# Batches 4, 5 and a tile of batch 3 turned to scoring all four experts, on a one-core state-read and expert-attention kernel

## The chip, the cores and the metric

The kernel runs on one core of a Trainium2 chip. The metric is the device time of one execution in microseconds (us). PE is the matrix engine, DVE the vector engine, ACT the scalar engine, POOL the general engine, and SP the engine on whose queue the DMA transfers are issued.

## The reference

Eight batches `x` of 8 heads, 512 tokens, 64 numbers each, and 32 state slots per head, are read against each other; the two results, 544 rows of 512 numbers per batch of which 512 are tokens, go through an attention layer with four experts, of which each row uses two.

```python
scores = scale * np.matmul(x, state.transpose(0, 1, 3, 2))   # tokens read the state
xread = np.matmul(softmax(scores), state)
scores2 = scale * np.matmul(state, x.transpose(0, 1, 3, 2))  # the state reads the tokens
sread = np.matmul(softmax(scores2), x)
x = concatenate([xread, sread])          # 8 batches, 544 rows, 512
logits = x @ w_gate                      # 4 experts, the 2 largest are kept
for e in range(4):
    q, k, v = x @ wq[e], x @ wk[e], x @ wv[e]
    a = softmax(causal(scale * (q @ k.T)))
    out += weight_of_e_for_this_row * (a @ v @ wo[e])
```

## The kernel before

The program is recorded first and emitted later. Each call to `st.mm`, `st.do`, `st.either` or `st.dma` records a step with the tiles that it reads and writes; `run` then emits all steps in the order that the constant `ORDER` holds, which also holds which of several engines does a step that more than one can do ("ways") and which buffer each tile gets. So nearly every instruction of the profile stands on one line, that of `run`, and is told apart by its tiles. On each engine instructions run in the order in which they were emitted. All transfers are issued on SP, before and after the change.

For each batch `front` makes, from tokens `xh` and their transposes `xT`, the scores against the state, softmax over 32 slots (`eb`, with maxima `mb` and sums `sbm`), its transposes `at`, the products `gs` of state and weights, and from these the values `v`, keys `kt`, queries and the weights of the gate (`wgt`). In batches 1 to 7 the softmax of the tokens comes from `state_scores`: two banks of PSUM (`sas`) hold all scores with tokens along a row, DVE turns them in blocks of 32 by 32 into `eb`, and the same banks give the state's own softmax `e2` with the maxima `m2`, which `side` goes on with (`a2`, `a2t`).

The causal attention of a batch works on four tiles of 128 tokens; tile `i` looks at `i + 1` blocks of 128 keys. `probs` does a unit of one or two tiles, in one of two ways:

- Sparse ("s"): each token has two slots, one for each expert that it uses. Queries are masked by slot into six columns of 64 (`m6`, `qf`, then a high and a low half-precision part in `qh`, turned by a DMA into `qm`). A tile has two lanes of scores. Each lane is the sum of a product over 128 rows of PE and one over 64 rows. `reads` multiplies each lane with the values of three experts (194 columns), weighs the result (`c`, `z`) and adds the slots' halves.
- Dense ("d", "0", "1"): all four experts are scored. Queries come out of PE already turned and are only split in two parts, `qm`. A tile has four lanes; a lane's products run over 64 rows, and two of them, on the upper and the lower half of PE, run side by side. `reads` multiplies each lane with one expert's values (65 columns), and a row's weight is zero for experts that it does not use.

In both, every product is made three times, of high and low parts. Each lane's scores go through DVE (a masked copy to `p` with its maximum `mx`), ACT (exponential), a split into `ph` (high part on ACT mostly, low part on POOL or DVE), a DMA that turns `ph` into `pt`, and `reads` on PE. Which way a tile goes is set by two numbers, `D1` and `DA`:

```python
def units_of(b):
    if b < CFG["D1"]:
        units = [((0, "s"), (1, "s")), ((2, "s"),), ((3, "s"),)]
    elif b < CFG["DA"]:
        units = [((1, "d"),), ((0, "s"), (2, "s")), ((3, "s"),)]
    else:
        units = [((1, "d"),), ((0, "0"), (2, "0")), ((0, "1"), (2, "1")), ((3, "0"),), ((3, "1"),)]
    return units
```

Before, both are 6: batches 0 to 5 are sparse, 6 and 7 dense. `tail` does the state's rows of two batches at a time, `result` the last product, of which the result leaves through `o`. `FILL` is a list of times at which a matmul on zeros (`band`) keeps PE at work in the first microseconds.

Of the kernel before, what the change touches and what calls it, by code (L numbers as in the profile page):

```python
# [21 lines left out]
ORDER = (
    (
        "c-jrs1A7n(7(n6AU$tu4EiBu{vTfV87nW_?wr$(CZR6hGaGvKqfshB%K{iMNksuWmg2<2_GC~oE00kivM1(|;8=^u6%nJYr1PlTS2_X%n$6S"
        "yMazI=Nf|aluih)6V2mps@um%!9bchGBAqFgk<xmb{LUD)#1uzfRfN)S2GC(XSh&ACjlz{S(1xrE&s0AUI6SCq7s0d{s8=izhSQ~O+VMqa$A"
        "U`C90&oiQVm_=4r{N4#fjV#wqCjbA2vy-M)P?hq6RW{as0Y>I0_4I*5FYBoMQ9AA;1V>4+_(oWLj!07`yoGGfo`x5u0mUA2`iu-WW<iJ8?s{"
        "y*adr`Gqi#u&>k}30cZlNpfxCMhRn#c4CZ48=mgDREA)WExD6KI7U&L%p&wj>BG?-iVrFOx*I@&MLLayR{b4aK!i~@u%Ht;ZLc`%Gtc3wE5s"
        "Kn55L$vGU?3F3xiAQpVi*+1o=^b?1JN=Z0+XR4?tr1N9DBhqSO+WcCQN|wkPoK7JXnccU^YyGRTz!BLJ6D-+hHV(hB+__ronvpOwnmNjDZDE"
        "3B%J&h(Tjv2F!v6I1Uy=1X_&?p(HlMdk{dCF(R#pHMj(-;987CO|T{|f~t5Q9zs)m1dZ@DM5e}A3Lii-ERA*XF+73iPz(3-GYF(=_y%r48N3"
        "Z&APPmLJ5Uzy!c%w))$s+C!*}o=YG7*E$F(s#e1MnG4Zp!hsE1#nBi2WwHuwoTqf>Hdj^E)kq=j(Q4(nhi?2bKf9k#_E&;t8mZw$pg*dKpFU"  # L30
        "pxo{uqO`0$v6oA(QgXF!Pp)r;t=eGf2bvPz@ZqEUcq`ChU0M~PC(#E*achREbNL?ur;Ql88{Ua&}<xzKj<$_!<qOC5>jf~fTQvM<Q$8B!yNn"
        "zBQOmG(R7SWV{jz?1H)06mj1w8+=S_9EXJj5G!6mNQyhwk@yHP|5ydCw#551X;ZNF({U|4e$0QUB4?zSBCBmc>8-wX92{UG=WV9V~(>4^`f&"
        "ti{lAvO8%104#0R5tGl!7ARR?I{B={xPfIJgs2QZC9syKo?7q}_M`<KiC7M0sg1=Ag)U7*66o%uE|)5FNxr7)Hv6F$?YG!E_YM(-DlwS;;sW"
        "R-$7Vi9;Yf??>n37>)z+G@inw7=Z(L4+molip=paIyUAwoD8F2R%pV39G6dE6&gYnC^<IeiWDDPQZqh-QMfdvz<7KPTTydPfUW5m$LFYgk~c"
        "|ZDo$rO8lU3A)P@pbN<7PFu`1odR9KDLQb{UG=lD1mp)yo}&SOd_MOok_w%}rPnuk*fx{U?tFyFyiRGlv2U93U(ur{^i)L4@`&=Iafudpn2q"
        "Pp}NL#Q6T!J$;2-eLn9Nv${t8&V^>jE(6EHlcPDo!iq@Y(_D77&WDibb>omb9#s6=mL(RYuJ-U(NTVng{TW1;1SfFdQk!%O=Br0C*yGx3>Wb"
        "rU&jd)i^o%I?n)DB67`^jJedx05O<^4oRWLf2mFYMI2GT(Db$Dd%T!9v)95_!k<^@m6Z1B?%<cFqrsE4doo?a`O2T_35nklJbd8hp6~4~j@C"
        "GlXnbd}R+a-R?!TgB#Ng95_SNRj($Miglo^o4`ipwZ1=aQY0TPkp<e#aGblk-S>UP%vdIpviYn1OHcDw<83D4(pQb@T&Q(@*@2b7;G)p)^>L"
        "f8l0YPY-dI?54z+k)QDfs>F|Q3*F|ev|BdI0V&IOcq8qhEwY`q%3jLBcexxt=X;!o^Gi<7!rSPe<mKO(7Q;(cE+9K-F71#AQh@i-A3Q)isXC"
        "YE`<#pOaW*c*^C+Se<m_CJ3v&qP<|6!pBTGTa#LuuO@26s1oJ(+iF3B%>7e$h)T#5svG|#8!ScWTeX0F2rsR~!)2mBZpP+hLUued%Rl83yIY"  # L40
        "Vs3&#|`+f)Z)+lo?ml_eB&c>P2O-r{)->DHh<xd{GE%!89FM*<PaU9<MNeH$S1x{jrb^?rNnxS&e3_gD*ZHxUYDf$50BFwIzeywq}-(+d`eE"
        "zVY){h_yYani*%n((G3aKLNZEKI`RX$DV_NbKcp^vi8`@MU%n+p<T7<-lb?K=!pRpLq^BjBcH^WHru}$`{^sr+%02lCB^RL48Z2j|j~107JX"
        "{M)GC@kNLv@V);}n`g`g5T4;6*e-QO-(A?Zqi&06(W;97P6lZ~puL)ECnrCW#^E<hG1dmj0R!i%A%tmlqUOVoEfLB`;}!W|a#vl!s|?c|{lH"
        "HKmh*8eL*b8tKDv<c`FZCG>_;X*>~$F9{^EB$OaYC6{EdCX&=LoHNT^Nh{gp1|^Zfd|A@VTY5wp<SLbvD{_+_Q${HvS!4v4l6Q2C9!hB`BQG"
        "$urq!{UT}E<QxhLf$lT77wI#J8ZBN?anC5JqbDVjzr$S5AokL5j8lqLLB#_I&lDV3zMEYPuBMW$+1c|z4>n)b5lGLDB?Q+Z0mZIUkK@jSwo@"
        "dRF|%XuPC*A+aCpUEw%A(OR}JdkGcTx!a6ZXqw_wJy>bI)j_bVvV3J<tcWN7xGG0@)DiN-(|4P)KHtnAE=d#;ej@Z+sb5K#Y=TI_m)A{R|B+"
        "-%;7iMS+3Jtox;zkt1Q!ZT1)!KT<#_xX*IW#)-p@q>ra`jKjgi%m)g?bKFdexD;;DFe~{PmMY_uy=^+tyj)qx3`6L_otNfBs8Dax0lJ=Kx@="
        "tzCPua*rt&c6_$XZAK$Z`dJE1S5ktk8GTQBeQNT3*DYo0;{4))UdbrfTXMPJ2l-UB}@yiq6&e8dX1PbPd$Fx`pFu3{9Z(xSuWNm^x2C>3m(O"
        "v2=|l)Yv-G*6V!UsH=2?9@DiNq+@N9)|XK>N*YK*IjLK8oXxS(c3R`;Y8_*9t&wcj(K1E`$atG6iFB+?wBy=X2Fe5*CtG!$?$h-=OPa_eyJ?"
        "^Gluou=c0zC4Y}v}`b&B1w{W?eP+IX2O6C_MB=_CE3gJm0U=ghi;Gw3`yq#5<G4w3niMTg2f8zkBFh%S&PnoWnve9NQXG>0D0`<hkr>2NuyI"  # L50
# [1164 lines left out]
```

## Time and profile before

| | us |
| --- | --- |
| Median of 3 runs (lowest to highest) | 283.56 (283.14 to 284.71) |
| The profiled execution, and its span from first to last instruction | 284.73, 283.0 |
| PE busy | 270.7 (96%) |
| DVE busy | 252.9 (89%) |
| ACT busy | 230.5 (81%) |
| POOL busy | 170.2 (60%) |

Busy time is that in which an engine has at least one instruction in it. Matmuls follow each other closer than each one lasts, so a busy PE is not yet PE at its peak; what a run of matmuls costs is read from its length.

### The profile page before, as it was taken

The page shows a single profiled execution, that of the slowest core. Times are in us where ns is not written, and L with a number is a line of the kernel's source. Part 1 is how long each engine was busy: PE and PEld are TensorE (multiplying, and loading weights), DVE is VectorE, ACT ScalarE, POOL GpSimd, SP SyncE. Part 2 cuts the span into 40 slices and gives each one's busy share as a digit, 9 for nine tenths or more (in the row PEclk, how much of TensorE's full clock was granted, in tenths as well). Part 3 has the DMA queues.
Part 4 walks back from the last instruction along what each step waited for, and adds up shares of the span by engine and source line. Part 5 has one row for each costly group of instructions (what it writes and reads, how often), then busy time and mean ns, then how long its engine had stood idle before and what let it go on. Part 6 is the DMA issues. An engine that isn't in the chain of part 4 may idle for free.

```text
span 283.0 us, 9152 instructions
## 1 busy us (share of the span) xinstructions
PE 270.7 (96%) x3406; PEld 182.6 (65%) x3407; DVE 252.9 (89%) x795; ACT 230.5 (81%) x624; POOL 170.2 (60%) x246
## 2 busy tenths in 40 slices
...
GB/s 197 237 107 157 182 195 177 195 218 171 179 173 193 145 186 292 192 201 135 238 197 183 190 201 230 141 203 209 133 152 164 226 147 199 122 184 188 209 227 244
DMA packets 161804, 53.16 MB, mean 188 GB/s; under 512 B 140640, under 2 KB 157280, under 8 KB 161760
## 3 DMA queue, kind: packets, MB, share of 16 engines
...
## 4 chain that ended last, share of the span: by engine, by line
PE 68%; DVE 19%; ACT 6%; issue 3%; DMA 2%; SPq 1%; POOL 0%; DVEq 0%; ACTq 0%
PE bank L266 68%; DMA xn<-in_x_dram 2%; DVE eb L266 2%; DVE xh L266 1%; DVE qf L266 1%; DVE sbm L266 1%; DVE gs L266 1%; DVE mb L266 1%; DVE p L266 1%; DVE z L266 1%; DVE a L266 1%; DVE ph L266 1%; SPq L266 1%; DVE m L266 1%; DVE et L266 1%
## 5 line engine op out<-in xcount | busy, mean ns | idle before, releaser
L266 PE MATMUL bank<-gs,at 128*128 128x260 f16 (+3 forms) x320 | 44.8, 284 | 1.4 <-DVE kt L266 0.8
L266 ACT ACTIVATE p<-p,mx 128x256 f32<-128x256 f32 (+3 forms) x80 | 41.8, 554 | 2.8 <-DVE mx L266 1.7
L266 PE MATMUL bank<-v,pt 128*128 128x194 f16 (+1 forms) x600 | 42.1, 226 | 0.5 <-DVE mx L266 0.4
L266 PE MATMUL bank<-kt,qm 64*128 64x128 f16 (+7 forms) x384 | 42.3, 298 | 0.2 <-DVE kt L266 0.2
L266 PEld LDWEIGHTS <-pt 128*128 128x128 f16 x600 | 38.3, 97 | 5.2 <-issue 2.9
L266 DVE CUSTOM_DVE_ANT_0 p<-bank,band 128x384 f32<-128x384 f32 (+3 forms) x80 | 36.4, 481 | 0.7 <-PE bank L266 0.3
L266 POOL TENSOR_TENSOR ph<-p,ph 128x1024 f16<-128x1024 f32 (+1 forms) x17 | 32.8, 1930 | 5.7 <-ACT ph L266 5.1
L266 PEld LDWEIGHTS <-at 128*128 128x128 f16 x288 | 27.3, 97 | 9.3 <-issue 2.9
L266 PEld LDWEIGHTS <-qm 64*128 64x128 f16 (+1 forms) x384 | 21.0, 95 | 17.1 <-issue 7.6
L266 PE MATMUL bank<-at,gs 128*128 128x512 f16 (+1 forms) x116 | 29.3, 395 | 0.7 <-ACT gs L266 0.7
L266 PE MATMUL bank<-wo_n,z 128*128 128x512 f16 (+1 forms) x114 | 26.2, 368 | 0.0
L266 ACT ACTIVATE ph<-p 128x1024 f16<-128x1024 f32 (+1 forms) x21 | 20.3, 965 | 0.4
L266 POOL TENSOR_TENSOR qh<-qf,qh 128x768 f16<-128x768 f32 x10 | 17.1, 1719 | 4.9 <-ACT qh L266 4.9
L266 PE MATMUL bank<-wo_n,zp 128*128 128x512 f16 x84 | 19.9, 379 | 0.0
L266 ACT ACTIVATE o<-bank 128x512 f32<-128x512 f32 (+1 forms) x27 | 15.4, 575 | 4.9 <-PE bank L266 2.7
L266 DVE SCALAR_TENSOR_TENSOR xh<-xn,xh 128x512 f16<-128x512 f32 x26 | 18.3, 705 | 0.0
L266 POOL TENSOR_TENSOR eb<-eb,sbm 128x512 f32<-128x512 f32 x14 | 15.1, 1077 | 5.1 <-DVE gt L266 2.4
L266 PEld LDWEIGHTS <-gs 128*128 128x128 f16 x108 | 10.2, 98 | 11.5 <-issue 1.1
L266 PEld LDWEIGHTS <-xh 128*128 128x128 f16 x416 | 14.4, 99 | 4.1 <-DVE xh L266 2.1
L266 PEld LDWEIGHTS <-z 128*128 128x128 f16 x114 | 10.3, 98 | 10.1 <-issue 1.1
L266 ACT ACTIVATE gs<-bank 128x260 f16<-128x260 f32 (+3 forms) x32 | 15.2, 499 | 1.1 <-PE bank L266 1.1
L266 ACT ACTIVATE xh<-xn 128x512 f16<-128x512 f32 x24 | 14.7, 629 | 1.2 <-DMA xn<-in_x_dram 1.1
(246 smaller groups left out, 668.2 us busy)
## 6 DMA issues: line engine op xcount, KB each, us to landing
...
pt<-ph SPq DMA_TRANSPOSE x28, 4.7
...
```

The lines of the kernel that those rows point to most:

```text
L266: f(**{k: v.ap() if isinstance(v, View) else v for k, v in kw.items()})
```

## The change

`D1` goes from 6 to 3 and `DA` from 6 to 4: batches 4 and 5 become dense, and in batch 3 tile 1 does. In `front` a bank's scores are turned by one DVE instruction of 512 columns where two of 256 stood. In `state_scores` the two maxima are scaled together, and both exponentials come behind that. `FILL` has an eleventh entry. `ORDER` is another one throughout.

```diff
-CFG = dict(FILL=(1.0, 1.4, 1.8, 2.2, 2.6, 3.0, 3.4, 3.8, 4.2, 4.6,), RA=-1, ...
+CFG = dict(FILL=(1.0, 1.4, 1.8, 2.2, 2.6, 3.0, 3.4, 3.8, 4.2, 4.6, 5.0,), RA=-1, ...
...
-           n_eb=1, n_e2=1, ..., n_pt=3, D1=6, DA=6)
+           n_eb=1, n_e2=1, ..., n_pt=3, D1=3, DA=4)
...
-                for k in range(2):
-                    st.do("DVE", 0.345, nc.vector.transpose, out=eb[:, u * 2 * H + k * H:u * 2 * H + (k + 1) * H],
-                          in_=sas[u][:, k * 256:(k + 1) * 256].rearrange("p (r q) -> p q r", r=2))
+                st.do("DVE", 0.62, nc.vector.transpose, out=eb[:, u * 2 * H:(u + 1) * 2 * H],
+                      in_=sas[u].rearrange("p (k r q) -> p k q r", k=2, r=2))
...
         for g, sa in enumerate(sas):
             dve(512, nc.vector.tensor_reduce, out=m2[:, g:g + 1], in_=sa, axis=AX.X, op=ALU.max, negate=True)
-            small(1, m2[:, g:g + 1], m2[:, g:g + 1], 0.0, 2.0 ** -17)
+        small(2, m2, m2, 0.0, 2.0 ** -17)
+        for g, sa in enumerate(sas):
             act(512, e2[:, g], sa, AF.Exp, bias=m2[:, g:g + 1], scale=2.0 ** -17, accum_out=s2[:, g:g + 1])
```

What this does to the instructions, counted over the whole program: on PE 132 products of 128x194 (`bank<-v,pt`) give way to 264 of 128x65, and 48 query products of 128x256 to 24 of 128x512; the score products (`bank<-kt,qm`) stay as many, but in the tiles concerned all run over 64 rows. DVE does 98 masked copies of scores where it did 80, and 12 turns of 512 columns where it did 24 of 256. ACT does 98 exponentials for 80. Nine tiles' query masks (`qf`) go, two thirds of them from ACT. On SP, `pt<-ph` transfers of 16 blocks of 128 columns go from 16 to 26 and those of 12 blocks from 12 to 6; `qm<-qh` transfers of 12 blocks go from 10 to 5, and one of 10 blocks comes.

The first place is PE at batch 4's `reads`, as its first tile begins (`v1` holds batch 4's values, `pt` the turned probabilities). Before:

```order
L266 LDWEIGHTS qm_0_133
L266 MATMUL bank_7_84<-kt_2_137,qm_0_133 128x128
L266 LDWEIGHTS pt_1_158
L266 MATMUL bank_1_78<-v1_0_107,pt_1_158 128x194
L266 LDWEIGHTS pt_1_158
```

After:

```order
L267 LDWEIGHTS tq_0_196
L267 MATMUL bank_6_83<-tk_0_191,tq_0_196 128x128
L267 LDWEIGHTS pt_1_158
L267 MATMUL bank_4_81<-v1_0_107,pt_1_158 128x65
L267 LDWEIGHTS pt_1_158
```

Each product has a third of the columns, there are twice as many, and each still has its own load of weights.

The second place is DVE where batch 4's scores begin to be copied out of their banks (`ISA p32,mx<-bank,band` is the masked copy, the `ISA mx` behind it reads its maximum). Before, the rows hold the first unit, tiles 0 and 1, of two lanes each:

```order
L266 STREAM_TRANSPOSE eb_0_115<-bank_6_83 128x256
L266 TENSOR_TENSOR z6_2_168<-bank_4_81,c6_0_173 128x384
L266 TENSOR_SCALAR su_2_171<-bank_5_82 128x2
L266 TENSOR_TENSOR ptl_0_201<-p32_2_114,ptl_0_201 128x640
L266 ISA p32_1_113,mx_3_163<-bank_0_77,band_66 128x128
L266 ISA mx_3_163 128x1
L266 RECIPROCAL su_2_171<-su_2_171 128x2
L266 ISA p32_1_113,mx_3_163<-bank_0_77,band_66 128x256
L266 ISA mx_3_163 128x1
L266 TENSOR_REDUCE mb_0_116<-eb_0_115 128x16
L266 TENSOR_TENSOR c6_3_176<-su_2_171,wgt_1_125 128x6
L266 ISA p32_1_113,mx_3_163<-bank_3_80,band_66 128x128
```

After, tile 1 has a unit of its own with four copies of 128x256, and behind it the next unit begins, among the turns of a later batch:

```order
L267 TENSOR_REDUCE m2_1_146<-bank_2_79 128x1
L267 STREAM_TRANSPOSE eb_0_115<-bank_4_81 128x512
L267 TENSOR_REDUCE m2_1_146<-bank_4_81 128x1
L267 ISA p32_1_113,mx_2_162<-bank_0_77,band_66 128x128
L267 ISA mx_2_162 128x1
L267 TENSOR_TENSOR gt2_0_129<-lg_1_123,gs1_1_132 128x20
L267 ISA p32_1_113,mx_2_162<-bank_3_80,band_66 128x128
L267 ISA mx_2_162 128x1
L267 SCALAR_TENSOR_TENSOR xh_1_94<-xn_2_89,xh_1_94 128x512
L267 RECIPROCAL su_0_169<-su_0_169 128x2
L267 ISA p32_1_113,mx_2_162<-bank_3_80,band_66 128x384
```

The copies for one batch go from eight to twenty, the two maxima `m2` stand close together, and one turn of 512 columns stands between them.

The third place is SP's queue while batch 4's probabilities are turned. Before, the queue turns two units of 12 blocks and then batch 5's masked queries:

```order
L266 DMA_TRANSPOSE pt_1_158<-ph_1_156 128x12x128
L266 DMA_TRANSPOSE pt_0_157<-ph_0_155 128x12x128
L266 DMA out_0_dram<-o_2_179 128x512
L266 DMA_TRANSPOSE a2t_0_151<-a2_0_152 128x8x128
L266 DMA_TRANSPOSE qm_0_133<-qh_1_141 128x12x128
L266 DMA_TRANSPOSE qm_0_133<-qh_0_140 128x12x128
```

After, there is no `qm` transfer, and every unit has 16 blocks:

```order
L267 DMA_TRANSPOSE pt_1_158<-ph_0_155 128x16x128
L267 DMA out_0_dram<-o_3_180 128x512
L267 DMA out_0_dram<-o_1_178 128x512
L267 DMA_TRANSPOSE a2t_0_151<-a2_0_152 128x8x128
L267 DMA_TRANSPOSE pt_2_159<-ph_1_156 128x16x128
L267 DMA_TRANSPOSE z_0_181<-zh_0_183 128x4x128
L267 DMA_TRANSPOSE pt_0_157<-ph_0_155 128x16x128
```

The number of turned transfers stays about the same; each of these is longer.

## Rows read from the trace of the kernel before

**Rows 1.** The page, busy time of each engine, share of the span, instructions.

```profile
PE 270.7 (96%) x3406; PEld 182.6 (65%) x3407; DVE 252.9 (89%) x795; ACT 230.5 (81%) x624; POOL 170.2 (60%) x246
```

**Rows 2.** The page, the chain that ended last, shares of the span by engine.

```profile
PE 68%; DVE 19%; ACT 6%; issue 3%; DMA 2%; SPq 1%; POOL 0%; DVEq 0%; ACTq 0%
```

**Rows 3.** Windows: busy time (and instructions) of each engine in two stretches.

```profile
core 0: us, PE busy (x) PEld busy (x) DVE busy (x) ACT busy (x) POOL busy (x), PEclk, DMA share, GB/s
40.00:100.00 60.00, 57.55 (x745) 38.91 (x745) 58.10 (x179) 55.71 (x159) 41.66 (x57) 1.00 1.05 183
125.00:232.00 107.00, 106.25 (x1377) 72.73 (x1376) 101.82 (x332) 88.98 (x260) 74.94 (x88) 1.00 0.96 185
```

**Rows 4.** Timeline of PE: scores of batch 5 and batch 6; start, length, count.

```profile
195.78 1.75 PE L266 MATMUL bank<-kt,qm 128*128 128x128 f16 x24
...
199.93 1.73 PE L266 MATMUL bank<-kt,qm 128*128 128x384 f16 x12
...
203.57 2.21 PE L266 MATMUL bank<-kt,qm 128*128 128x512 f16 x12
...
213.00 0.83 PE L266 MATMUL bank<-kt,qm 64*128 64x256 f16 x12
...
225.07 1.48 PE L266 MATMUL bank<-kt,qm 64*128 64x384 f16 x24
...
230.92 1.47 PE L266 MATMUL bank<-kt,qm 64*128 64x512 f16 x12
```

**Rows 5.** Timeline of PE: `reads` of a sparse tile and of a dense tile.

```profile
160.12 2.17 PE L266 MATMUL bank<-v,pt 128*128 128x194 f16 x24
...
253.09 1.63 PE L266 MATMUL bank<-v,pt 128*128 128x65 f16 x48
```

**Rows 6.** The page, groups: scores to probabilities; count, busy, mean ns, idle before.

```profile
L266 ACT ACTIVATE p<-p,mx 128x256 f32<-128x256 f32 (+3 forms) x80 | 41.8, 554 | 2.8 <-DVE mx L266 1.7
...
L266 DVE CUSTOM_DVE_ANT_0 p<-bank,band 128x384 f32<-128x384 f32 (+3 forms) x80 | 36.4, 481 | 0.7 <-PE bank L266 0.3
L266 POOL TENSOR_TENSOR ph<-p,ph 128x1024 f16<-128x1024 f32 (+1 forms) x17 | 32.8, 1930 | 5.7 <-ACT ph L266 5.1
...
L266 ACT ACTIVATE ph<-p 128x1024 f16<-128x1024 f32 (+1 forms) x21 | 20.3, 965 | 0.4
```

**Rows 7.** Groups by form: masked queries, their two parts, low parts of probabilities on DVE.

```profile
L266 POOL TENSOR_TENSOR qh<-qf,qh 128x768 f16<-128x768 f32 x10 | 17.1, 1719 | 4.9 <-ACT qh L266 4.9
...
L266 ACT ACTIVATE qf<-bank,m 128x64 f32<-128x64 f32 x42 | 9.2, 335 | 0.7 <-POOL m L266 0.4 <-PE bank L266 0.2
...
L266 ACT ACTIVATE qh<-qf 128x768 f16<-128x768 f32 x11 | 9.1, 849 | 0.7 <-DVE qf L266 0.7
L266 DVE TENSOR_TENSOR qf<-bank,m 128x384 f32<-128x384 f32 x17 | 9.0, 546 | 0.5 <-POOL m L266 0.2
...
L266 DVE TENSOR_TENSOR ph<-p,ph 128x1024 f16<-128x1024 f32 x7 | 8.6, 1225 | 0.2 <-ACT ph L266 0.2
```

**Rows 8.** Groups by form: full banks copied by ACT and DVE, and turns on DVE.

```profile
L266 ACT ACTIVATE o<-bank 128x512 f32<-128x512 f32 x25 | 14.6, 590 | 4.6 <-PE bank L266 2.4 <-DMA out_dram<-o 2.1
...
L266 DVE STREAM_TRANSPOSE eb<-bank 128x256 f32<-128x256 f32 x24 | 9.7, 428 | 0.1
...
L266 DVE STREAM_TRANSPOSE et<-eb 128x512 f32<-128x512 f32 x12 | 8.4, 702 | 0.1
...
L266 DVE TENSOR_SCALAR o<-bank 128x512 f32<-128x512 f32 x8 | 5.5, 683 | 0.7 <-PE bank L266 0.4
```

**Rows 9.** Groups by form: weight loads from `pt`, idle time before them and its ends.

```profile
L266 PEld LDWEIGHTS <-pt 128*128 128x128 f16 x600 | 38.3, 97 | 5.2 <-issue 2.9 <-DMA pt<-ph 0.2
```

**Rows 10.** The page, transfers: count, median us from issue to landing.

```profile
pt<-ph SPq DMA_TRANSPOSE x28, 4.7
```

More of the change, by code (lines that the diff above doesn't have):

```diff
@@ L29 @@
[L29 to L38, printed above, removed]
@@ new lines @@
+        "O^IK+oUunc0t8Yl+|AP2045>Os0Kn~1;p>P6LK~Ag=6(JYafRa!E!yq@*gi}xna$_k-50xP+X2U#K1x`YCtOYqC9E67mP!&!?Z8!txpbjL4s"
+        "8A3uKwT&U)t~|7#X{H!8p3&~2dm*MG=ut37V_amxCDFQGBk(MP#CX3YiI#iAwRZ+4zLdnKwG#5%V7&-#IBGDTR|Jhj7lA08>EHq&<^&)0^9{"
+        "eTcH~?hK;ZY`vOxESO=S7A-0F2cpVBtFW3N0U@`87B3J;LLT~5?H=sW(!9H*kHbD=V1WWNC41fyQ2}Zy`SPw#jAQbb!2igP0a3l<d&QKhOz)"
+        "%<l!(j?+hh>-?4naj+j&ooF9EB1%5q834*vl($6ikI3a0`0ET*wR4U?q-*c`zMH;wlWJFdPH7AsWqxQkVk5(;cXUr7<%E(E^wOWpEaBfxEB}"
+        "Dr0o2fiqz&)W>@;8*1V>h(gJrERKg-SOv@BeW;Dcpgex0!;lXm(jsV#4e%j6fJjso7sC>G1Wm9ZMy1EF8japSMtB0%a4A&B$g~C<VN>jY&mj"
@@ new lines @@
+        "UiwZ^A#1fIbQcnfQ>8P>s<@D94-duWcY-~)Vx0BVEX@gsD@<M0VOVqffqy|D%M!@3xbK0{mVfqn2be24zn347u<sD}ga2V{qV_yyMCARLTCa"
+        "3~JL&Nu~s&~N$)KWR92!LKv{C*mL4h%sm?expe^8~@Q{Y>6?c9ZthvG!tV{d;Ciya1O?%^%#dX;Vhhv-^sBR#-owA0q0_T8iW5}2L1xzd6<H"
+        "J19Bz`A;54Lmk`6_C?t%4F)=HQ#RN1TGt(akz=Xs&4o71a%1Vi7JZ{Fnkdk^*ER2nDFfsL_RFs6WQBsPFsi_P_#BI10vy)(N+K%xs4MoCFw4"
+        "3|T0aVOE@i8q0Q(yW_>F5h3qnxw_6W~5Rh`EUP5GKS>N{TyhHzp^;$QX!+F+Cl{lb8yQAae%lNBwC4<%eS!j?2?7JdS%%cqb;pV9ZS!N!d6&"
+        "pFrnRm<&r$1=@>csQ}gGAl@ZKC^1Io2%H@E;Xn%DQdEyqV0|t}r!fZa$B0~rDpDS5zzw-59paKyn9kr3Do8;X0+DzS9p#h|nZxKXpXO$imx|"
```

79 lines of the change are left out of this document (42 added, 37 removed).

## The prediction

> **What bounds the kernel now.** I read the page's busy times first: PE is at work in 96% of the span, DVE in 89%, ACT in 81%, POOL in 60% [rows 1]. The chain that ended last agrees: 68% of it lies on PE, 19% on DVE, 6% on ACT [rows 2]. These are averages over stages, so I then cut the span into windows [rows 3]. From 40 to 100 us DVE is busiest: 58.10 of 60 us, 96.8%, with PE at 57.55 and ACT at 55.71 (92.8%). From 125 to 232 us, where the attention of batches 3 to 5 is done, PE is busy for 106.25 of 107 us, DVE for 101.82 (95%), ACT for 88.98 (83%), POOL for 74.94 (70%). So the stretch that the change reworks is bound by PE, with DVE 4.4 us behind it and ACT 17 us behind. What the change is worth there is what PE loses, until DVE or ACT ends last.
>
> **PE.** Scores: the three units of sparse batch 5 take 1.75 + 1.73 + 2.21 = 5.69 us, the units of dense batch 6 take 0.83 + 1.48 + 1.47 = 3.78 us [rows 4]. A batch turned dense gives back 1.91 us, two give 3.8, and tile 1 of batch 3, with 2 of a batch's 10 blocks, 0.4: together 4.2 us. `reads`: 24 products of 194 columns last 2.17 us, 90 ns each, and 48 of 65 columns last 1.63 us, 34 ns each [rows 5]. Away go 132 x 90 ns = 11.9 us, in come 264 x 34 ns = 9.0 us: 2.9 us back. The query products have the same columns before and after (48 x 256, 24 x 512), so nothing. PE: 7.1 us less. Each run's length holds the end of its last product, which overlaps what follows, so 6.5 is the lower end. The loads of weights for 132 more products are hidden already: the 34 ns include them.
>
> The 34 ns carry this term, since the products become short [rows 5]. The gain of both parts, 7.1 us, would be gone if a short product cost (11.9 + 4.2) / 264 us = 61 ns. [...]
>
> **DVE.** In: 18 masked copies at 36.4/80 = 0.455 us = 8.2 [rows 6]; five low parts of 1024 columns at 1.23 = 6.1 [rows 7]; four low parts of dense queries, priced as a full bank at 0.69 = 2.8 [rows 8]. Out: three low parts of 768 columns (three quarters of 1.23) = 2.8; four query masks at 9.0/17 = 0.53 = 2.1; six results of 384 columns at the same price less two of 256 = 2.4; two low parts of queries = 1.9 [rows 7]; four outputs at 0.69 = 2.8, which the order gives to ACT; and the turns, 24 x 0.404 = 9.7 against 12 of 512 columns. The nearest row for those is the turn of 512 columns between buffers, 8.4/12 = 0.70 [rows 8], which makes 8.4, so 1.3 less; reading from a bank it could cost as much as two halves, and then nothing is won. I take 1.3. So far DVE has 3.8 us more. The new order moves small work off it: low parts of `at`, scalings, sums of slot halves, small copies, some fifty groups too small to show; by my count of them with their own durations these come to 6 us less. I take DVE as 2 us lower, with 4 us higher as the other end, if that relief falls outside the stretch.
>
> **ACT.** In: 18 exponentials at 41.8/80 = 0.52 = 9.4; four more high parts (eight of 1024 columns in, four of 768 out) at 0.97 = 3.9 [rows 6]; eight full banks (four of queries, four outputs) at 0.58 = 4.6; ten pieces of results priced like the masks' pieces, 0.22 each = 2.2. Out: 30 mask pieces at 9.2/42 = 0.22 = 6.6, five high parts of queries at 0.83 = 4.1 [rows 7, 8]. That is 9.4 us; with the small work that comes from DVE, 10 us more.
>
> **POOL.** Two low parts of probabilities more, 3.9 us, three of queries less, 5.1 [rows 6, 7]: no change.
>
> **SP.** The turned transfers stay as many, but carry 160 + 10 - 72 - 60 = 38 blocks more. A `pt` transfer has 14.3 blocks on average and lands after 4.7 us [rows 10], 0.33 us a block at most; 38 blocks would be 12.5 us if nothing overlapped, zero if the queue has room. It has: in the whole run the weight loads waited 0.2 us for `pt` [rows 9]. I take zero. No transfer changes its queue.
>
> **Small edits.** The first exponential of `e2` now waits for the second bank's maximum, a DVE pass of about 0.69 us [rows 8], at most 7 x 0.69 = 4.8 us over the batches if ACT had nothing else to do; behind it in ACT's queue stand other batches' exponentials, and `e2` is needed only by `side`, so I take zero, and the seven small scalings saved are as little. One more warming product costs 0 to 0.4 us.
>
> **The sum.** In the stretch of 107 us PE comes to 106.25 - 7.1 = 99.2, DVE to about 99.8, ACT to about 99. PE can run at 99% (it does now), and DVE has been run at 96.8% from 40 to 100 us [rows 3]. DVE then ends last: 99.8 / 0.968 = 103.1 us, 3.9 less than 107. The rest of the program keeps its work. The profiled execution of 284.73 us becomes 280.8; that execution lies 1.2 us above the median of the three runs, 283.56, from which the same 3.9 us give **279.7 us**.
>
> **Rivals.**
> *PE alone decides* (the forecast's lower end): if the order finds cover for DVE as it has for PE, the full 7.1 us come out, 276.5. For it speaks that DVE's work can still move to POOL, which is 30% idle; against it, that POOL is slow at it, 1.93 us for a low part that takes DVE 1.23 [rows 6, 7].
> *DVE takes all back*: the work that dense tiles must have on DVE falls in the stretch, the relief outside. DVE comes to 101.82 + 3.8 = 105.6 us there, and even at 99% that is 106.7: 283.3. [...] The trace before shows DVE 4.4 us behind PE, so there is little room.
> *ACT becomes the bound, and the kernel slower*: ACT goes from 88.98 to 99 us in the stretch, and each lane's exponential stands between DVE's maximum and the transfer of `pt`. From 40 to 100 us ACT ran at 92.8%; at that share 99 us need 106.7, no change. The point that decides is 99/107 = 92.5%: if ACT reaches only 90% because its work comes in bursts behind DVE's maxima, the stretch takes 110 us and the kernel 286.6. Against it: ACT's largest groups hardly wait, 2.8 and 0.4 us in all [rows 6].
> *Short products cost 61 ns in this stretch*: PE keeps its 106.25 us and nothing is won, 283.6. Against it stand the 34 ns of the same products later in the run [rows 5]. [...]
> *The transfers end last*: a third of the 12.5 us uncovered would give 4.2 us, and take the whole gain: 283.9.
> *The change doesn't do what it says* can be left out: the rows of the order show the dense products and the long turns.
>
> **How the numbers follow.** The forecast with its lower end gets 0.62, and by itself 276.5 to 282 us; DVE takes all back 0.18; ACT 0.13; short products 0.02; transfers 0.05. A measurement of this kernel can tell about 0.5%, 1.4 us, from no change: faster means below 282.1. The forecast lies there, and a quarter of the DVE rival, which goes from nothing won to half: 0.67. The rest of that rival, the short products, the transfers and some of ACT's near end make 0.21 for no difference, and ACT's far end 0.12 for slower. The range for 8 in 10 goes from 276.2 to 284.0: down to PE alone, up through the rivals near no change.
>
> **What would show it.** The scores of batches 4 and 5 should take 3.8 us a batch, and 48 short products 1.6 us. In the stretch of batches 3 to 5 PE's busy share should fall below that of before and DVE's rise to about 97%. A turn of 512 columns from a bank should last near 0.70. If ACT or `pt` stand among what PE's loads wait for, with more than 2 us, the rivals have it; if PE's share stays at 99% and the time falls by 7 us, PE alone decided. Wrong altogether would be a stretch before 100 us that changes by more than 2 us, since only the order differs there.

## The result, and the profile after

The change made the kernel slower: 285.74 us, the median of 13 runs (284.86 to 287.46), against 283.57 before on the same chip (282.97 to 284.92). The ratio is 1.0069, with an interval of 1.0049 to 1.0089, some 2 us. The prediction was 279.7 and faster. The profiled execution after took 285.42 us, its span 283.6. Runs in which PE's mean granted clock was 1.000 are 1 to 2 us faster than those at 0.993 or 0.994, in both kernels: after, 7 have a median of 285.42 us and 6 one of 286.44; before, on the chip of the first experiments, 8 have 283.25 and 15 have 285.00.

The page of the changed kernel: busy time of each engine, the chain that ended last, and a group of POOL's.

```profile
PE 264.7 (93%) x3516; PEld 172.2 (61%) x3516; DVE 253.6 (89%) x776; ACT 238.7 (84%) x642; POOL 176.2 (62%) x252
...
DVE 22%; PE 18%; ACT 5%; DMA 3%; issue 3%; POOL 2%; DVEq 0%; ACTq 0%; POOLq 0%
...
L267 POOL TENSOR_TENSOR ph<-p,ph 128x1024 f16<-128x1024 f32 (+1 forms) x19 | 38.9, 2048 | 12.4 <-ACT ph L267 8.5
```

PE is busy for 6.0 us less than in [rows 1], where 7.1 were forecast. But the span is 0.6 us longer, so PE stands idle for 283.6 - 264.7 = 18.9 us, where it was 283.0 - 270.7 = 12.3. Between the two profiles 6 us are won on PE and 6.6 us lost in waits. The chain says the same: of PE's 68% in [rows 2], 18% are left, and other engines and gaps have the rest.

Not all of the 6 us come from the change. The first two rows are of the kernel before, a window and one run of products in it; the third is the same run of products after. In a window's row the second number is the length, then come the busy times of PE, PEld, DVE, ACT and POOL, and then PE's granted clock.

```profile
17.10:20.60 3.50, 3.48 (x48) 2.81 (x50) 2.63 (x9) 2.89 (x12) 0.88 (x2) 0.51 0.18 41
...
17.52 1.11 PE L266 MATMUL bank<-p,bd 64*32 64x256 f32 x16
...
16.52 0.66 PE L267 MATMUL bank<-p,bd 64*32 64x256 f32 x16
```

Before, PE stood idle for 1.94 us until 17.05, waiting for `xh` of DVE, and then its granted clock was 0.51 on the mean from 17.1 to 20.6 us. Four runs of products in there take 1.11 + 0.31 + 1.11 + 1.06 = 3.59 us, the same four after the change 0.66 + 0.24 + 0.63 + 0.62 = 2.15. So some 1.4 of the 6.0 us are the clock's, an estimate from these rows, and 4.6 are left for the change. With these 1.4 us the spans of the two profiles differ by 2.0 us and not by 0.6, near the 2.2 of the medians.

Where the waits are is read from windows. First the kernel before, stretches that were not shown yet.

```profile
0.00:40.00 40.00, 35.15 (x451) 25.43 (x453) 29.52 (x74) 31.25 (x75) 19.74 (x55) 0.96 0.77 179
...
100.00:200.00 100.00, 98.51 (x1232) 67.46 (x1231) 95.42 (x301) 85.56 (x251) 72.19 (x88) 1.00 1.04 198
200.00:240.00 40.00, 40.00 (x461) 25.23 (x460) 37.60 (x131) 32.42 (x80) 24.10 (x32) 1.00 0.86 168
240.00:284.00 44.00, 39.49 (x524) 25.55 (x521) 32.25 (x115) 25.58 (x64) 12.53 (x18) 0.99 0.89 194
```

The same windows after, and the stretch of 125 to 232 us that the prediction reckoned with:

```profile
0.00:40.00 40.00, 35.79 (x497) 25.25 (x499) 32.30 (x79) 31.53 (x72) 24.23 (x55) 1.00 0.92 189
40.00:100.00 60.00, 55.41 (x728) 37.54 (x724) 57.66 (x168) 54.26 (x157) 40.23 (x55) 1.00 0.96 178
100.00:200.00 100.00, 97.89 (x1284) 62.20 (x1283) 94.30 (x298) 91.30 (x250) 81.26 (x103) 1.00 1.13 203
125.00:232.00 107.00, 101.62 (x1427) 64.60 (x1425) 100.71 (x325) 96.49 (x267) 76.39 (x95) 1.00 1.06 197
200.00:240.00 40.00, 36.35 (x499) 21.87 (x494) 37.40 (x121) 34.04 (x96) 20.82 (x27) 1.00 0.90 183
240.00:284.00 44.00, 39.24 (x521) 25.36 (x519) 31.99 (x114) 27.59 (x72) 9.66 (x15) 1.00 0.96 194
```

Length less PE's busy time is PE's idle time in a stretch (before, [rows 3] for the second; the last ends with the span, at 283.0 and 283.6):

| stretch, us | PE idle before | after | more |
| --- | --- | --- | --- |
| 0 to 40 | 4.85 | 4.21 | -0.64 |
| 40 to 100 | 2.45 | 4.59 | 2.14 |
| 100 to 200 | 1.49 | 2.11 | 0.62 |
| 200 to 240 | 0.00 | 3.65 | 3.65 |
| 240 to the end | 3.51 | 4.36 | 0.85 |

From 100 to 200 us, where batch 4 is done densely and batch 5 begins, PE waits only 0.6 us more, though DVE and ACT are at 94% and 91% there. All of its idle time in there is 2.1 us, so neither of the two can have cost more than that. The loss is in 200 to 240, where PE does the `reads` of batch 5 while batch 6 begins, and in 40 to 100, where, but for the long turns, only the order differs. From 200 to 240 us DVE is no busier than before (37.40 us, before 37.60). In the 107 us that the prediction reckoned with, of which 200 to 232 is a part, PE's idle time goes from 0.75 us [rows 3] to 5.38. So something else than the load of DVE or ACT ended last.

What it is the timeline shows; the columns are start, length, engine, operation, and in brackets the idle time ahead with what ended it. First PE's scores of batch 4 and `reads` of its dense tiles, the terms that the prediction priced:

```profile
150.98 0.83 PE L267 MATMUL bank<-kt,qm 64*128 64x256 f16 x12
...
155.11 0.83 PE L267 MATMUL bank<-kt,qm 64*128 64x384 f16 x12 [0.17 <-DVE xt_tail L267]
...
161.87 0.83 PE L267 MATMUL bank<-kt,qm 64*128 64x384 f16 x12
...
169.88 0.82 PE L267 MATMUL bank<-kt,qm 64*128 64x512 f16 x6
...
175.19 0.82 PE L267 MATMUL bank<-kt,qm 64*128 64x512 f16 x6
180.32 1.64 PE L267 MATMUL bank<-v,pt 128*128 128x65 f16 x48
```

They are as forecast from [rows 4, 5], but for the scores standing in five runs and not in three: 4.13 us for batch 4, not 3.78. Now the places of three waits, all engines:

```profile
58.36 1.65 POOL L267 TENSOR_TENSOR qh<-qf,qh 128x768 f16<-128x768 f32 x1
58.44 2.12 DVE L267 SCALAR_TENSOR_TENSOR xh<-xn,xh 128x512 f16<-128x512 f32 x1
...
210.07 2.13 POOL L267 TENSOR_TENSOR ph<-p,ph 128x1024 f16<-128x1024 f32 x1 [1.01 <-ACT ph L267]
210.14 2.09 DVE L267 SCALAR_TENSOR_TENSOR gt<-gt,gt 128x16 f32<-128x16 f32 x1
212.16 0.41 DVE L267 SCALAR_TENSOR_TENSOR v<-bank,v 128x256 f16<-128x256 f32 x1
212.62 0.59 PE L267 MATMUL bank<-wo_n,zp 128*128 128x512 f16 x2 [1.45 <-DVE v L267]
...
220.44 0.75 POOL L267 TENSOR_SCALAR mx<-mx 128x4 f32<-128x4 f32 x1
220.44 0.68 DVE L267 CAST ph<-p 128x1024 f16<-128x1024 f32 x1
221.19 1.21 DVE L267 TENSOR_TENSOR ph<-p,ph 128x1024 f16<-128x1024 f32 x1
221.25 1.21 POOL L267 TENSOR_TENSOR c<-su,wgt 128x4 f32<-128x4 f32 x1
222.50 0.93 ACT L267 ACTIVATE z<-bank,c 128x64 f32<-128x64 f32 x4 [1.50 <-POOL c L267]
223.47 0.40 PE L267 MATMUL bank<-wn,bd 64*32 64x260 f16 x10 [1.11 <-ACT z L267]
```

At 210.14 a DVE instruction on 16 columns lasts 2.09 us, from just behind the start of POOL's low part of `ph` to its end; the nine instructions `gt<-gt,gt` of this profile last 0.17 us at the median. Behind it in DVE's queue stands `v`, late, and for `v` PE waits 1.45 us. At 220.44 it is the other way round: POOL's `mx` and `c`, four columns each, last as long as DVE's work on `ph` beside them, 0.75 beside 0.68 and 1.21 beside 1.21; elsewhere in this profile most of them take 0.19 to 0.20. For `c` ACT waits 1.50 us, and PE 1.11 us for ACT. At 58.44 `xh` lasts 2.12 us beside a low part of `qh` on POOL that began 0.08 us ahead of it; where it isn't held it takes 0.67 (a profile below).

So a DVE instruction that reads two operands from SBUF (`gt`, `xh`, the low part of `ph`), or copies within it (the CAST of `ph`), and an instruction of POOL exclude each other in these rows: one of them waits until the other has ended, and its wait counts into its own length: 2.09 us beside 2.13 us, 0.75 us beside a cast of 0.68. A `v` with one operand from a bank isn't held further below: it lasts 0.42 us in the midst of a low part of POOL's. The program marks such steps itself, in `takes_port` (from which the expectations have the word port; what the two engines share no run shows), so the prediction could have looked for them.

Such meetings aren't new with the change. Take what a DVE instruction lasts beyond its usual length (such that a tenth of the same instruction's records in all kept traces are shorter), and add it up where POOL is at work beside it and more than 0.2 us are over. By this sum DVE is held for 5.2 us in the kernel before, in 16 pieces of at most 0.88 us, and for 6.8 us in the changed kernel, in 8 pieces, of which two last 1.93 and 1.49. What is new is a few long ones ahead of steps that PE waits for.

### The profile page after: what moved, and what is told of

It is laid out like the page before. It is cut to its first block, busy times and chain, and to the rows that moved or that the text cites. A ratio compares the mean times of both kernels' runs of the same rounds, so it can differ in the third digit from the quotient of the medians.

```text
span 283.6 us, 9372 instructions
## 1 busy us (share of the span) xinstructions
PE 264.7 (93%) x3516; PEld 172.2 (61%) x3516; DVE 253.6 (89%) x776; ACT 238.7 (84%) x642; POOL 176.2 (62%) x252
## 4 chain that ended last, share of the span: by engine, by line
DVE 22%; PE 18%; ACT 5%; DMA 3%; issue 3%; POOL 2%; DVEq 0%; ACTq 0%; POOLq 0%
PE bank L267 18%; DVE p L267 5%; DMA pt<-ph 3%; DVE ph L267 2%; ACT p L267 2%; DVE gs L267 1%; DVE gt L267 1%; DVE v L267 1%; DVE eb L267 1%; ACT z L267 1%; DVE xh L267 1%; DVE kt L267 1%; DVE m L267 1%; DVE sbm L267 1%; POOL xh L267 1%
## 5 line engine op out<-in xcount | busy, mean ns | idle before, releaser
L267 ACT ACTIVATE p<-p,mx 128x256 f32<-128x256 f32 (+3 forms) x98 | 51.1, 557 | 1.9 <-POOL mx L267 1.0
L267 POOL TENSOR_TENSOR ph<-p,ph 128x1024 f16<-128x1024 f32 (+1 forms) x19 | 38.9, 2048 | 12.4 <-ACT ph L267 8.5
L267 DVE CUSTOM_DVE_ANT_0 p<-bank,band 128x256 f32<-128x256 f32 (+3 forms) x98 | 43.8, 479 | 0.7 <-PE bank L267 0.4
L267 PE MATMUL bank<-v,pt 128*128 128x65 f16 (+1 forms) x732 | 39.0, 210 | 1.2 <-DMA pt<-ph 0.6
L267 PE MATMUL bank<-gs,at 128*128 128x260 f16 (+3 forms) x272 | 38.2, 287 | 0.0
L267 PE MATMUL bank<-at,gs 128*128 128x512 f16 (+1 forms) x140 | 34.8, 391 | 0.4 <-DVE tmx L267 0.4
L267 ACT ACTIVATE z<-bank,c 128x64 f32<-128x64 f32 x64 | 14.4, 317 | 3.1 <-POOL c L267 2.7
L267 ACT ACTIVATE gs<-bank 128x512 f16<-128x512 f32 (+3 forms) x35 | 16.7, 499 | 0.0
L267 POOL TENSOR_TENSOR c<-su,wgt 128x6 f32<-128x6 f32 (+1 forms) x24 | 5.8, 240 | 16.3 <-DVE su L267 14.3
L267 POOL TENSOR_TENSOR at<-et,at 128x512 f16<-128x512 f32 x10 | 12.3, 1235 | 5.4 <-DVE at L267 5.1
```

The costliest lines, as they stand in the source:

```text
L267: f(**{k: v.ap() if isinstance(v, View) else v for k, v in kw.items()})
```

## The experiments

The theory to test, called the holds here: the lost time comes from meetings of DVE and POOL instructions that exclude each other, which the new order sets at places where PE waits. Its rivals: DVE's work ends last (the prediction's own step); ACT's work does, in bursts; or a dense configuration can't be ordered as well. All ratios are to the kernel before on the same chip; the changed kernel's is 1.0069. Taken against its runs at a granted clock of 1.000 alone, the ratios of the experiments would be 0.2 to 0.5% higher, all those of one chip by the same. Where the edit is in the table of the order, the diff shows rows of an engine's order.

**The gate behind the values.** In the order alone three small steps on DVE, and the ACT step that follows them, move behind batch 6's `v`, so that `gt` isn't ahead of `v` when POOL begins its low part.

```diff
 TENSOR_TENSOR cmp<-cmp,over 128x80
-SCALAR_TENSOR_TENSOR gt<-gt,gt 128x16
 SCALAR_TENSOR_TENSOR v<-bank,v 128x4x64
 TENSOR_SCALAR su<-bank 128x4
-TENSOR_REDUCE gs<-gt 128x4
 RECIPROCAL su<-su 128x4
-RECIPROCAL gs<-gs 128x4
 SCALAR_TENSOR_TENSOR v<-bank,v 128x4x64
 SCALAR_TENSOR_TENSOR kt<-bank,kt 128x512
 SCALAR_TENSOR_TENSOR v<-bank,v 128x4x64
+SCALAR_TENSOR_TENSOR gt<-gt,gt 128x16
+TENSOR_REDUCE gs<-gt 128x4
+RECIPROCAL gs<-gs 128x4
```

> The changed kernel with one move in the order: four small steps of batch 6's gate (gt, gs, gs, gs) stand behind two low parts of v and one of kt instead of ahead of them on DVE. Theory A (held port): in the changed kernel DVE's gt of 128x16 lasts 2.09 us beside POOL's low part ph of 2.13 us, v waits behind it, and PE stands still 1.6 us at 212.6 us and 0.5 us at 214.5 us; with the move these go and the kernel takes 1.5 to 2.1 us less than the changed kernel's 285.7, so 283.6 to 284.2. Theory B (the dense tiles' added work on DVE and ACT holds PE wherever it stands): the same time, 285.2 to 286.2, with the idle time of PE moved elsewhere.

Measured: 0.9934 (0.9902 to 0.9967), 282.44 us, less than the 283.6 to 284.2 that were expected; span 280.7. The timeline at the place:

```profile
208.37 2.14 POOL L263 TENSOR_TENSOR ph<-p,ph 128x1024 f16<-128x1024 f32 x1 [1.00 <-ACT ph L263]
208.44 0.42 DVE L263 SCALAR_TENSOR_TENSOR v<-bank,v 128x256 f16<-128x256 f32 x1
...
209.31 1.46 PE L263 MATMUL bank<-wo_n,zp 128*128 128x512 f16 x6
...
210.30 0.25 DVE L263 SCALAR_TENSOR_TENSOR gt<-gt,gt 128x16 f32<-128x16 f32 x1
```

`v` runs beside POOL at its usual length, and PE runs on without a wait. Its windows:

```profile
40.00:100.00 60.00, 57.08 (x744) 38.77 (x744) 58.10 (x172) 56.21 (x163) 42.61 (x57) 1.00 1.03 184
...
200.00:240.00 40.00, 37.91 (x544) 23.12 (x543) 37.25 (x128) 35.23 (x97) 21.25 (x25) 1.00 1.01 188
```

The gain in span is 2.9 us, more than the wait removed: 1.56 us come in 200 to 240, and 1.67 us in 40 to 100, where nothing was edited. There `xh` took 0.67 us in this kernel, and POOL's second `qh` was held in its place. Which of the two is held differs between kernels at nearly the same starts (POOL's 58.36 and DVE's 58.44 us above, 58.23 and 58.30 below), so part of any gain here can belong to that tie and not to the edit.

**Clear of POOL.** The same, and the two small POOL steps at 220 us go elsewhere in the order: `c` to DVE, ahead of its work on `ph`, and `mx` to ACT.

```diff
 POOL
-TENSOR_SCALAR mx<-mx 128x4
-TENSOR_TENSOR c<-su,wgt 128x4
 DVE
+TENSOR_TENSOR c<-su,wgt 128x4
 CAST ph<-p 128x1024
 ACT
 ACTIVATE z<-bank,c 128x64 x4
+ACTIVATE mx<-mx 128x4
```

> As the kernel with the gate moved, and two small steps taken from POOL: c of one tile to DVE and mx of one unit to ACT. In the changed kernel they took 1.21 and 0.75 us instead of 0.20 at 220.4 to 222.4 us, beside DVE's CAST of ph and low part of ph, and PE stood still 1.27 us at 223.5 us for the z that waits for c. Theory A: 1.0 to 1.3 us less again than with the gate moved alone, 282.4 to 283.2, so no slower than the kernel before. Theory B: 285.2 to 286.2.

Measured: 0.9878 (0.9834 to 0.9921), 280.19 us, less than the 282.4 to 283.2 that were expected; span 278.6. It is faster than both kernels: its runs, all at a granted clock of 0.999 or more, are 3.1 us below the 283.25 of those before at 1.000. Its timeline at the tie and at the place of the two small steps:

```profile
58.23 2.26 POOL L263 TENSOR_TENSOR qh<-qf,qh 128x768 f16<-128x768 f32 x1
58.30 0.67 DVE L263 SCALAR_TENSOR_TENSOR xh<-xn,xh 128x512 f16<-128x512 f32 x1
...
216.82 0.15 DVE L263 TENSOR_TENSOR c<-su,wgt 128x4 f32<-128x4 f32 x1
...
217.39 0.93 ACT L263 ACTIVATE z<-bank,c 128x64 f32<-128x64 f32 x4
...
219.00 0.53 PE L263 MATMUL bank<-wn,bd 64*32 64x260 f16 x24
```

Neither ACT's `z` nor PE's products behind it have a wait in brackets any more, and at 58.30 it is POOL that is held: its low part lasts 2.26 us, not 1.65, though it began 0.07 us ahead of `xh`. The window of 200 to 240 us:

```profile
200.00:240.00 40.00, 39.28 (x571) 24.04 (x571) 37.97 (x135) 36.64 (x104) 20.40 (x24) 1.00 1.00 191
```

PE's idle time in 200 to 240 goes from 3.65 to 0.72 us. With PE at 263.9 us of work, 14.7 us of idle time are left in all. Every instruction of the dense way is still done, so the gain on PE was there, and most of it was spent on waits that this order can do without. How much of it is the tie's is taken up below.

**Less work for DVE.** In the changed kernel DVE does only 64 columns of the low parts of batch 4's and 5's values, keys and queries. The rest of these low parts, 5.3 us of DVE, is left out.

```diff
+        if now["b"] in (4, 5) and lo.buf.tag in ("v0", "v1", "v2", "kt", "qm"):
+            k = 1 if lo.buf.tag[0] == "v" else 64
+            hi, lo, src = hi[:, :k], lo[:, :k], src[:, :k]
```

> The changed kernel, in which DVE makes the low parts of v, kt and qm of batches 4 and 5 for 64 columns only (the other columns keep what the buffers held): 5.3 us of DVE's work left out between 125 and 232 us, nothing else. Theory B with DVE as the engine that holds PE's banks: 2 to 4 us less, 282 to 284. Theory A alone (events at 210 to 224 us only): at most 1 us less, unless the times of the two engines shift past each other there. If neither DVE's nor ACT's load bounds the stretch: same time.

Measured: 1.0012 (0.9983 to 1.0041), span 282.4, 0.57% less than the changed kernel. If DVE ended last, most of 5.3 us (1.9%) would have come out. In its profile `xh` wasn't held at 58 us (0.67 us), and 11 of its 12 runs are at a granted clock of 0.997 or more, so this run by itself shows no gain from DVE's work.

**Less work for ACT.** In the changed kernel ACT makes the high part `ph` of batches 4 and 5 for 256 columns only, where its eight instructions had 1024 each; 5.1 us of ACT are left out. The diff is cut down to the call; in `split` the new argument cuts the columns of ACT's instruction.

```diff
-        split(n, ph[:, :n], ph[:, n:2 * n], p32[:, :n])
+        split(n, ph[:, :n], ph[:, n:2 * n], p32[:, :n], 256 if b in (4, 5) else None)
```

> The changed kernel, in which ACT makes the high parts ph of batches 4 and 5 for 256 of 768 or 1024 columns only (the rest keeps what the buffer held): about 5 us of ACT's work left out between 125 and 232 us, nothing else. If ACT's added exponentials are what gives the gain of PE back, 2 to 4 us less, 282 to 284. Theories A and B with DVE: less than 1 us less, 284.7 to 286.

Measured: 1.0099 (1.0065 to 1.0133), slower than the changed kernel, which no theory had expected. Its timeline has new holds, of which one is shown:

```profile
216.50 2.14 POOL L263 TENSOR_TENSOR ph<-p,ph 128x1024 f16<-128x1024 f32 x1 [0.16 <-ACT ph L263]
216.59 2.08 DVE L263 TENSOR_TENSOR wgt<-gt,gs 128x16 f32<-128x16 f32 x1
...
219.75 0.42 PE L263 MATMUL bank<-a2t,xh 128*128 128x64 f16 x9 [1.39 <-DVE mx L263]
```

Less work on ACT moved the meetings and made other small DVE steps long, as `wgt` here, of which the changed kernel's two on DVE last 0.17 and 0.30 us: by the sum above DVE is held for 8.8 us, in the changed kernel for 6.8. A gain from ACT's work doesn't show. By itself this run can't exclude one that the new holds hide; the 2.1 us of idle time that PE has from 100 to 200 us bound it there. That the new holds are the whole of the loss is argued from the rows, not shown by a run.

**Low parts in halves.** POOL's low part of `ph` in the changed kernel as two instructions of half the columns. If a hold lasts for an instruction, it halves.

```diff
-        st.either([("POOL", 0.147 + n * 0.001887, (nc.gpsimd.tensor_tensor, kw)), ...
+        h = n // 2
+        parts = [dict(out=lo[:, a:a + h], in0=src[:, a:a + h], in1=hi[:, a:a + h], op=ALU.subtract) for a in (0, h)] if lo.buf.tag == "ph" else [kw]
+        st.either([("POOL", 0.147 + n * 0.001887, *((nc.gpsimd.tensor_tensor, k) for k in parts)), ...
```

> The changed kernel, in which each low part of ph that POOL makes is two instructions of half the columns, one behind the other, in the same place; the order is untouched. Theory A (a DVE instruction with both operands in SBUF waits until POOL's running instruction ends): DVE's gt at 210 us is held for 1.1 us at most, not 2.09, and PE's idle time there falls by about 1 us: 284.2 to 285.2, against 285.7 of the changed kernel. If the hold does not go by the instruction but by the work (both halves back to back), gt stays near 2.1 us and the time at 285.2 to 286.2. What POOL pays for 19 instructions more, about 0.1 us each, has room in its 38% idle time.

Measured: 1.0077 (1.0051 to 1.0102), 286.35 us: no better than the changed kernel, and not the 284.2 to 285.2 that were expected. The timeline:

```profile
54.09 1.63 DVE L263 SCALAR_TENSOR_TENSOR xh<-xn,xh 128x512 f16<-128x512 f32 x1
...
60.00 1.64 POOL L263 TENSOR_TENSOR qh<-qf,qh 128x768 f16<-128x768 f32 x1 [1.10 <-ACT qh L263]
60.06 2.13 DVE L263 SCALAR_TENSOR_TENSOR xh<-xn,xh 128x512 f16<-128x512 f32 x1
...
212.24 2.27 POOL L263 TENSOR_TENSOR ph<-p,ph 128x512 f16<-128x512 f32 x2 [1.63 <-ACT ph L263]
212.31 1.13 DVE L263 SCALAR_TENSOR_TENSOR gt<-gt,gt 128x16 f32<-128x16 f32 x1
...
213.83 1.46 PE L263 MATMUL bank<-wo_n,zp 128*128 128x512 f16 x6 [0.49 <-DVE v L263]
```

At the place itself it went as the holds have it: `gt` lasts 1.13 us, half of POOL's pair, and PE waits 0.49 us, not 1.45. But `xh` was now held at two other places, beside low parts of POOL's that weren't halved (`xh`, `qh`), and nothing was won in all.

**The long turn undone.** In the kernel that is clear of POOL, the turn of 512 columns as two of 256 in the same step.

```diff
-                st.do("DVE", 0.62, nc.vector.transpose, out=eb[:, u * 2 * H:(u + 1) * 2 * H],
-                      in_=sas[u].rearrange("p (k r q) -> p k q r", k=2, r=2))
+                st.either([("DVE", 0.62, *((nc.vector.transpose, dict(out=eb[:, u * 2 * H + k * H:u * 2 * H + (k + 1) * H],
+                      in_=sas[u][:, k * 256:(k + 1) * 256].rearrange("p (r q) -> p q r", r=2))) for k in range(2)))])
```

> The kernel with the gate moved and two small steps taken from POOL (280.2 us, 0.9878 of before), in which each turn of 512 columns is two of 256 again, in the same place. If the long turn was a cost of the change (it holds DVE for 0.70 us in one piece), 0.5 to 1.5 us less: ratio 0.983 to 0.986. If it is worth what the trace says, 12 times 0.1 us, and DVE is near the bound, 0 to 1 us more: ratio 0.988 to 0.992.

Measured: 0.9959 (0.9930 to 0.9988), 0.8% above the kernel that it starts from. Its profile lost the tie at 58 us (`xh` 2.06 us at 58.35), and soon behind that PE's granted clock fell:

```profile
66.00:68.00 2.00, 2.00 (x27) 1.25 (x27) 1.42 (x5) 2.00 (x10) 1.75 (x3) 0.52 1.13 211
```

So it didn't tell what the turns are worth; it is done again below.

**Orders searched by the same program.** To tell the configuration from its order, two kernels got an order, engines and buffers from one local search over durations taken from the traces: one dense as after, one with `D1` and `DA` at 6 as before.

```diff
-D1=3, DA=4
+D1=6, DA=6    # in the second of the two
```

> The changed kernel's steps with another order, choice of engines and buffers: a local search over a list of durations taken from the traces of before and of the changed kernel, with the rule that a DVE instruction with both operands in SBUF and a POOL instruction do not run at once. Theory A: with those meetings avoided all along, below the 280.2 us of the two edits by hand; 266 to 276. Beside the sparse kernel searched in the same way: if the dense tiles are worth what PE gives back, 4 to 7 us less than it; theory B (their work on DVE and ACT gives it back): within 1.5 us of it.

> The changed kernel's code with D1 and DA back at 6 (batches 0 to 5 sparse, as before), and an order searched in the same way and for the same time as that of the searched dense kernel, from the order of the kernel before. If the order alone made the changed kernel lose, this one gains as much on before as the dense one on the changed kernel, and stands 4 to 7 us above it: 271 to 281. Theory B: within 1.5 us of the searched dense kernel.

Measured: 1.0902 (1.0863 to 1.0941) and 1.0972 (1.0935 to 1.1009), where 266 to 276 us and 271 to 281 were expected. Neither is ahead: the intervals overlap, and the medians of all six runs stand the other way round, 316.64 and 314.16 us. Both are so far from the kernels in question that they say nothing about orders as good as these. What makes them so slow isn't shown; in their traces DVE is held for 20.4 and 15.8 us by the sum above, though the search had a rule against that, and in the dense one's PE waits 5.8 us for transfers of `qm`. What each configuration is worth under its best order stays open.

**The tied step sooner.** In the changed kernel `xh` goes ahead of a DVE instruction that stood before it. The tie at 58 us should then fall to DVE more often.

```diff
+SCALAR_TENSOR_TENSOR xh<-xn,xh 128x512
 TENSOR_REDUCE mb<-eb 128x16
-SCALAR_TENSOR_TENSOR xh<-xn,xh 128x512
```

> The changed kernel with one DVE instruction moved: xh of 128x512, which at 58.4 us begins 0.08 us behind POOL's second low part of qh and is held to 2.12 us there, stands one instruction earlier, ahead of the reduction mb, so that it waits about 0.5 us for POOL's first low part and has the port before the second. In the profiles of the kernels with the gate moved the same meeting went the other way (xh 0.67 us, PE idle 3.1 to 3.2 us between 60 and 80 us instead of 4.9). Theory A: if most runs of the changed kernel lose this meeting, 0.8 to 1.4 us less: ratio to before 1.001 to 1.004. If they mostly win it, or if the 1.45 us are hidden, 0 to 0.5 us more: 1.007 to 1.009.

Measured: 1.0023 (0.9999 to 1.0046), by the ratios 0.46% or 1.3 us less than the changed kernel, with that one row moved. But all of its runs are at a granted clock of 0.999 or more, and its 285.25 us are only 0.2 less than those of the changed kernel at 1.000, on another chip. One view of its timeline, and then its window:

```profile
58.66 1.02 DVE L263 SCALAR_TENSOR_TENSOR xh<-xn,xh 128x512 f16<-128x512 f32 x1
```

```profile
40.00:100.00 60.00, 56.83 (x743) 38.50 (x742) 58.07 (x172) 55.90 (x160) 41.42 (x59) 1.00 1.02 184
```

`xh` is held for 0.35 us and not for 1.45, and PE's idle time in 40 to 100 falls from 4.59 to 3.17 us, while the span falls by 0.6. So one such tie costs between 0.2 and 1.4 us; closer it isn't known.

**Clear of POOL, with the tied step sooner.** The same move in the kernel that is clear of POOL, as a base that doesn't hang on that tie.

> The kernel with the gate moved and two small steps taken from POOL (ratio 0.9878), and xh moved as in the run above. Theory A: the meeting at 58 us no longer goes one way in some runs and the other way in others, so a median about the same, 0.984 to 0.989, and fewer runs 1 to 3 us above the fastest.

Measured: 0.9913 (0.9881 to 0.9944). This missed its expectation: no gain over the kernel that it starts from, and four of six runs 1 to 3 us above the fastest (280.77 to 283.08). Its profile shows `xh` held for 1.29 us at 39.30, another tie earlier on. Taking one tie away doesn't take them all.

```profile
58.69 1.02 DVE L263 SCALAR_TENSOR_TENSOR xh<-xn,xh 128x512 f16<-128x512 f32 x1
```

Beside the run before it, though, it is the cleanest measure of the two places at 210 and 220 us: the same chip, a granted clock of 0.998 or more in all runs, and at 58 us `xh` held alike, for 0.35 us in both (this row and the one above). The one has the gate's steps moved and the two small steps taken from POOL, the other hasn't, and they take 282.21 and 285.25 us. The two places are worth 3.0 us, 1.1%.

**The two questions put again on that base.** First the two turns, then the cut of DVE's low parts (5.3 us left out again).

> As the run above, with each turn of 512 columns as two of 256 in the same place. On the kernel without xh moved this cost 0.8%, but its profile lost the meeting of xh at 58 us. If the turn itself is the price, 12 times 0.07 to 0.1 us of DVE's time: 0.3 to 1.0 us more than the run above, 0.1 to 0.35%. If two short turns cost more than that for another reason, 0.8% again.

> The kernel with gate, two small steps and xh moved, in which DVE makes the low parts of v, kt and qm of batches 4 and 5 for 64 columns only (the rest keeps what the buffers held): 5.3 us of DVE's work left out between 125 and 232 us. If DVE ends last in that stretch once the held steps are gone, as predicted, 1.5 to 3.5 us less than without the cut: 0.975 to 0.982. If PE or the transfers do, less than 0.7 us less.

Measured: 0.9903 (0.9872 to 0.9934) and 0.9898 (0.9868 to 0.9929), against 0.9913 of their base. The long turn is worth nothing that can be measured. And 5.3 us less for DVE give 0.15%. The windows of the base and of the cut one:

```profile
100.00:200.00 100.00, 97.87 (x1284) 62.20 (x1282) 94.32 (x298) 91.30 (x250) 81.30 (x102) 1.00 1.14 203
```

```profile
100.00:200.00 100.00, 97.85 (x1284) 62.00 (x1283) 90.81 (x297) 90.83 (x251) 81.13 (x101) 1.00 1.11 201
```

DVE has 3.51 us less to do in the stretch, and PE's 97.9 us don't move. In the dense stretch PE still ends last.

## Why the prediction was wrong

**The step that failed** is "DVE then ends last: 99.8 / 0.968 = 103.1 us, 3.9 less than 107", with "The rest of the program keeps its work". DVE's load didn't end last: with 5.3 us less of it the time stays (0.9898 against 0.9913), and PE's busy time from 100 to 200 us stays too. What ended last at the costly places were single steps of DVE and POOL that held each other while PE waited for them; without two such places 3.0 us come out. In the stretch of 107 us PE's idle time rose from 0.75 to 5.38 us, most of it between 200 and 232, and the 40 to 100 us, to which the sum gave nothing, lost 2.14. A sum that prices each instruction alone leaves both out. The prediction read the order at three places for what was issued, and not for which DVE and POOL instructions it puts side by side; no rival named such a meeting. Its own test, a stretch before 100 us that changes by more than 2 us, was met.

**PE, 7.1 us less:** the mechanism was right and the size too large. PE's busy time fell by 6.0 us between the profiles, of which some 1.4 are the clock's in the profile before; about 4.6 came from the change, below the 6.5 of the lower end. Short products cost 1.64 us for 48, 34 ns each, as taken; the scores of batch 4 came to 4.13 us and not 3.78, since they run in five pieces: twice 0.83 us where 24 products in one run took 1.48, and twice 0.82 where 12 took 1.47 [rows 4]. At that price two batches make 0.7 us of the difference. The rest of it stays open. The rival of short products at 61 ns is out.

**DVE, 2 us less:** it has 100.71 us in the stretch, 1.1 less than in [rows 3] and near the 99.8 forecast; its share there is 94%, not the 97% that was named as a sign, and what it was held for counts into that. The long turn lasts 0.706 us from a bank, as taken from [rows 8], but the 1.2 us that it saves DVE (8.5 against 9.7) aren't on the path.

**ACT, 10 us more:** it got 7.5 us more in the stretch, 96.49 in all. As a bound it is out from 100 to 200 us, where PE's idle time is 2.1 us in all. The rival's 286.6 us lie near the 285.74 measured, but by chance: it has the stretch wait for ACT's load, and what was found is 3.0 us at two places.

**POOL, no change:** the term that was mis-sized with consequences. Its busy time rose by 6.0 us: low parts of `ph` went from 17 of 1930 ns to 19 of 2048, and small steps were given to it, `c` 24 times where it was 18 and `mx` 8 where it was 5. More important, its instructions hold DVE's and are held by them (6.8 us of DVE by the sum above, 1.21 us for a `c`), so that its 60% was not free room.

**SP and transfers, zero:** PE's weight loads waited 1.4 us for `pt` in the whole run, 0.2 us before [rows 9], which is below the 2 us that were named as a sign, and 2.0 us for `z`: a little more than nothing.

**The small edits, zero:** no run speaks against it; the two turns measured nothing, and the order of the exponentials and the entry of `FILL` have no run of their own.

**The sum put right.** With the two places at 210 and 220 us cleared, and the tie at 58 us not lost, the profile's span is 278.6 us, 4.4 less than before: PE's work is 6.8 us less (270.7 - 263.9) and its idle time 2.4 us more (14.7 - 12.3). By the estimate above 1.4 of the 6.8 are the clock's, so 3.0 us are left, as the runs at a granted clock of 1.000 have it, 283.25 and 280.19. That this is near the 3.9 us of the forecast is chance, for it comes about in another way. The changed kernel's 6.6 us of added idle time aren't all accounted for: the two holds give 1.45 + 1.11 us of PE's waits, the stretch with the tie 1.4 us, and clearing them took 18.9 us to 14.7; the other 2.4 us stay open. So does why the tie at 58 us falls to POOL in the changed kernel and to DVE in others with the same order up to there.
